# Six small moves in a fused routing attention and mixture-of-experts kernel: sums, gathers, a scatter, first copies and a late value load

## The chip, the cores and the metric

The kernel runs on one core of a Trainium2 chip. The metric is the device time of one execution in microseconds (us). A core has five engines that run side by side and meet at semaphores: TensorE (PE, matmuls), VectorE (DVE), ScalarE (ACT), GpSimd (POOL, which also issues gathers and scatters) and SyncE (SP, which issues loads). Matmuls write to banks of PSUM; everything else lives in SBUF or in device memory.

## The reference, cut to what matters

Two blocks in a row. First, attention in which a query sees only the keys of its own cluster:

```
q, k, v: (4, 8, 768, 64)      centroids: (8, 16, 64)
q_assign = argmax(einsum(q_n, c_n));  k_assign = argmax(einsum(k_n, c_n))
scores   = where(q_assign == k_assign, q @ k.T / sqrt(D), -1e9)
attn_out = softmax(scores) @ v
x        = attn_out as (3072, 512)       # one row for each token
```

Then a mixture of 8 experts, of which each token takes one:

```
logits = x @ w_gate;  e = argmax(logits);  gate = softmax(logits)[e]
y[t]   = gate * (relu(x[t] @ w1[e]) @ w2[e])     # w1: 512x1024, w2: 1024x512 each
```

The tokens of an expert must be brought together (gather), multiplied by that expert's weights, and their rows put back (scatter).

## The kernel before, in words

**Attention.** There are 16 groups: four batches times four pairs of heads. A group has 12 units: two halves of the queries (`half`) by six blocks of 128 keys (`j`). `score(u)` puts a 128x768 tile of scores into one of three wide PSUM tiles (`sps`), ACT takes the exponential into a tile `A` (L1002), and DVE adds the tiles of a half into `T` (`add_up`: L1016 for the first two, L1020 for the rest), for the denominators. `attend(u)` multiplies `A` with the values into one of two banks `O` (L1034). Turn `n` of the main loop does the 12 scores of group `n`, then its 12 attends.

**Jobs between them.** The order of the work is written by hand. `at(n, part, f)` hangs job `f` into turn `n`: a number below 12 is the place behind that score, `UG + j` (with `UG` = 12) the place behind attend `j`, `mid` stands between scores and attends, `end` after the attends. Instructions go onto each engine's queue in exactly this order, and an engine never overtakes within its queue.

**Clusters.** Queries and keys of a group are turned: the first group by PE (`turn`, copied out of PSUM by DVE and ACT at L886, L887 and L891), later groups by DVE alone (`turn_blocks`, L897). `similar(g)` makes the similarities to the centroids on PE (L911) into a wide PSUM tile, which DVE turns (L918). `assign` and `assign2` find the cluster, and its one-hot goes into `ohT` (`put`, `put_q`, `put_by_scalar`), where it masks the scores (L1000). `idle` puts unneeded matmuls on PE while it would wait at the start.

**Experts, in the last turns of attention.** When three batches are done, the tokens of experts 0 and 1 from those batches are placed already. `tokens1` multiplies one-hots on PE into token numbers, which DVE turns into integers (`indices`, L698 to L712). `spread1` spreads these over the partitions (PE L719, DVE L698 to L726, into `g_idx`). `gather1(0)` has POOL fetch nine blocks of rows (L292). Nine of the 12 units of group 14 do not add up at once: they are kept in `later_sums`, which `sums_of_later` works off behind the gathers' issue. In turn 15, `turn_rows1(0)` divides the gathered rows (L305) and turns them (L308) for PE's first layer (L321).

**Experts after attention.** A list `groups` of 15 tiles is worked off: full tiles of experts 2 to 7 by a product scheme with seven half-size products (`layer1_s`, L498; `pair_s`, L520), the others by `layer1` (L321) and `layer2` (L386). Each has its rows gathered (`gather_of`, L292), divided (L305), turned (L308), multiplied, and scattered to the output (`rows_to`, L341). `sums_x` makes the sums of the turned rows (L408, L409) that L498 starts with. `adds[0]` is the postponed tail of a quarter-tile of expert 0: three DVE additions (L367, L371) and a scatter. Weights come as transfers of 2 MB from SP's queue (L236, L241), each when its buffer has been read for the last time.

**The end.** A number `xe[NX + 2]` says whether the inputs need the general path, which these inputs do not take. Every engine loads it into a register (`values_load`, L1460) and branches on it (L1461).

Of the kernel before, what the change touches and what calls it, by code (L numbers as in the profile page):

```python
# [8 lines left out]
F32 = mybir.dt.float32  # L9
# [176 lines left out]
def kernel(  # L186
# [11 lines left out]
    nc = tc.nc  # L198
    B, H, S, D = q.shape
    C = centroids.shape[1]  # L200
    P = 128
# [21 lines left out]
    NX = -(-(N - CAP) // P) + 1  # L223
# [43 lines left out]
    ps_o = late.enter_context(tc.tile_pool(name="ps_o", bufs=2, space=PSUM))  # L267
# [3 lines left out]
    def apart(first, second):  # L271

        first, second = (getattr(i, "ins", i) for i in (first, second))
        tc.declare_no_dep(second, first, reason="other banks and other elements")


    def wide():
        return pools["s"].tile([P, 2, 512], F32, name="sps")
# [4 lines left out]
    def bank():  # L283

        return wide()[:, 0, :] if "attention" in pools else ps_o.tile([P, 512], F32, name="O")

    def gather(g):

        n = 0
        for j, m in enumerate(g["n"]):  # L290
            for i in range(m // 32):
                nc.gpsimd.indirect_dma_start(  # L292
                    out=g["xg"][:, n, :], out_offset=None, in_=x_q[0 : 4 * g["rows"], :],
                    in_offset=bass.IndirectOffsetOnAxis(ap=g["gi"](j, i), axis=0),
                )
                n += 1
# [318 lines left out]
    xe = rte.tile([1, NX + 3], I32)  # L615
# [120 lines left out]
    with ExitStack() as actx:  # L736
# [79 lines left out]
        ps = bank()  # L816
# [44 lines left out]
        def blocks():  # L861
            cps = bank()
            nc.tensor.transpose(cps[:, 0:P], cn.rearrange("p a d -> p (a d)"), ident)
            cview = cps[:, 0:P].rearrange("p (g a c) -> p g a c", a=2, c=C)
            for a in range(2):
                nc.vector.tensor_copy(cblk[a * D : (a + 1) * D, :, a, :], cview[a * D : (a + 1) * D, :, a, :])
# [4 lines left out]
        def turn(g, piece):  # L871

            if piece == 0:
                qk[g] = qkp.tile([P, 2, S], F32, name="qk")
            n = NQ - 4 if piece else 4
            ps = wide().rearrange("p a c -> p (a c)")
            for i in range(2 * n):
                w, j = divmod(i, n)
                if i == n and piece == 0:
                    blocks()  # L880
                nc.tensor.transpose(
                    ps[:, w * 512 + j * P : w * 512 + (j + 1) * P], rows[g, "qk"[w]][:, 4 * piece + j].rearrange("p a d -> p (a d)"), ident
                )
            if piece == 0:
                apart(
                    nc.vector.tensor_copy(qk[g][:, 0, 0:512], ps[:, 0:512]),  # L886
                    nc.scalar.copy(qk[g][:, 1, 0:512], ps[:, 512:1024]),  # L887
                )
            else:
                for w, copy in enumerate((nc.vector.tensor_copy, nc.scalar.copy)):  # L890
                    copy(qk[g][:, w, 512:S], ps[:, w * 512 : w * 512 + n * P])  # L891

        def turn_blocks(g):

            qk[g] = qkp.tile([P, 2, S], F32, name="qk")
            for w in range(2):
                nc.vector.transpose(qk[g][:, w, :], rows[g, "qk"[w]].rearrange("p j a d -> p (j a d)"))  # L897
# [7 lines left out]

        def similar(g):

            ps = wide()[:, 0, :]
            for t in range(4):
                w, half = divmod(t, 2)  # L910
                nc.tensor.matmul(  # L911
                    ps[t * 2 * C : (t + 1) * 2 * C, 0:HS], lhsT=cblk[:, g % HP].rearrange("p a c -> p (a c)"),
                    rhs=qk[g][:, w, half * HS : (half + 1) * HS], start=True, stop=True,
                )


            sims[g] = asg.tile([P, HS], F32, name="sim")
            nc.vector.transpose(sims[g], ps[:, 0:HS])  # L918
# [64 lines left out]
        A, T, O = {}, {}, {}  # L983
        XT = {}

        def where(u):
            g, r = divmod(u, 2 * NQ)
            return g, r // NQ, r % NQ
# [21 lines left out]
        def add_up(u, a_u):  # L1010
            g, half, j = where(u)
            if j == 0:
                last_a[0] = a_u
            elif j == 1:
                T[g, half] = tp_.tile([P, 2, HS], F32, name="T", bufs=4)
                nc.vector.scalar_tensor_tensor(  # L1016
                    T[g, half], in0=last_a[0], scalar=1e-9 / P, in1=a_u, op0=ALU.add, op1=ALU.add
                )
            else:
                nc.vector.tensor_tensor(T[g, half], T[g, half], a_u, op=ALU.add)  # L1020

        later_sums = []

        def sums_of_later():
            for x in later_sums:
                add_up(*x)

        def attend(u):
            g, half, j = where(u)
            if j == 0:  # L1030
                O[g, half] = ps_o.tile([P, 512], F32, name="O")
            a_ = A.pop(u)
            for a in range(2):
                nc.tensor.matmul(  # L1034
                    O[g, half][a * D : (a + 1) * D, 0:HS], lhsT=rows[g, "v"][:, a, j, :], rhs=a_[:, a, :],
                    start=(j == 0), stop=(j == NQ - 1),
                )
# [92 lines left out]
        def at(n, part, f, *a):  # L1130
            jobs.setdefault((n, part), []).append((f, a))

        UG = 2 * NQ
# [10 lines left out]
        at(-3, mid, assign, 0)  # L1144
        at(-3, mid, assign2, 0)
        at(-3, mid, put, 0)
        at(0, 1, put_q, 0, 1)
        at(-2, end, idle_of, 20)
        at(-1, end, turn_blocks, 1)
        for f in (similar, assign, assign2):  # L1150
# [62 lines left out]
        n = NG - HP  # L1213
# [4 lines left out]
        at(n + 1, end, one_hots1, 1)  # L1218

        at(n + 2, UG + 3, tokens1)  # L1220
        at(n + 2, UG + 8, spread1)
        at(n + 2, UG + 8, gather1, 0)
        at(n + 2, UG + 8, sums_of_later)
        at(n + 3, mid, gather1, 1)
        at(n + 3, mid, turn_rows1, 0)

        n = NG
# [54 lines left out]
    with tc.tile_pool(name="sm", bufs=1) as sm:  # L1282
# [20 lines left out]
        for part in parts:  # L1303
            n, over = part["n"], part["over"]
            nc.vector.tensor_tensor(over, over, b2.unsqueeze(2).to_broadcast([P, E, n]), op=ALU.mult)
            more = sm.tile([P, NF], F32, name="more")[:, 0:n]
# [51 lines left out]
    def gather_of(g):  # L1358
        g["xg"] = pools["xg"].tile([P, NJ * 4 + 1, XQ], F32, name="xg")
        gather(g)  # L1360

    def turn_of(g):
        if "xT" not in g:
            g["xT"] = pools["wk"].tile([P, DB, CAP], F32, name="xgT")
        turn_rows(g)
# [7 lines left out]
    def static(e, j0):  # L1373
        c0 = e * (NJ + 1) + j0
        return dict(
            n=[P] * (NJ - j0) + [RQ], rows=N, e=lambda: e, gi=blocks_at(g_idx, c0), si=cols_of(s_idx, c0), apart=True, s=j0 == 0
        )
# [8 lines left out]
    groups = [static(1, 1)]  # L1386
# [3 lines left out]
    ng = len(groups)  # L1390

    def fetch1_of(i):
        groups[i]["e"] = groups[i]["e"]()
        groups[i]["w"] = [fetch1(groups[i]["e"], i + 1)]

    gather_of(groups[0])
    adds[0]()
    gather_of(groups[1])
    groups[0]["w"], groups[1]["w"] = weights[1], w_s
    g = groups[0]  # L1400
    g["xT"] = p1.tile([P, DB, CAP], F32, name="xu", bufs=1)
# [16 lines left out]
    layer2(g)  # L1418
    fetch1_of(2)
    for i, g in enumerate(groups):  # L1420

        n1 = groups[i + 1] if i + 1 < ng else dict(s=False)
        n2 = groups[i + 2] if i + 2 < ng else dict(s=False)
        if i + 1 < ng:
            n1["h"] = pools["wk"].tile([P, FB, CAP], F32, name="h_sb", bufs=2)
            steps = [lambda: divide_rows(n2)] if i + 2 < ng else []
            if i == 0:
                steps.append(lambda: turn_of(n2))
            if n1["s"]:
                layer1_s(n1, steps)  # L1430
            else:
                for f in steps:
                    f()
                layer1(n1, (0, FB))
        if i + 3 < ng:
            fetch1_of(i + 3)
        if i + 2 < ng:
            if i > 0:
                turn_of(n2)
            if i + 4 < ng:  # L1440
                gather_of(groups[i + 4])
        steps = sums_w1(n2) + sums_x(n2) if n2["s"] else []
        if n1["s"]:
            for f in sums_h(n1) + sums_w2(n1):
                f()
        if g["s"]:
            pair_s(g, steps)
            layer2(g, range(2, len(g["n"])))
        else:
            for f in steps:  # L1450
                f()
            if i > 0:
                layer2(g)
        if i + 2 < ng:
            n2["w"].append(fetch2(n2["e"], i + 3))
# [1 line left out]

    mctx.close()
    late.close()
    more = nc.values_load(xe[0:1, NX + 2 : NX + 3], min_val=0, max_val=2)  # L1460
    with tc.If(more > 0):  # L1461
        nx = nc.values_load(xe[0:1, NX : NX + 1], min_val=0, max_val=NX)
        general = nc.values_load(xe[0:1, NX + 1 : NX + 2], min_val=0, max_val=1)
        with tc.If(nx > XU):
            with ExitStack() as ectx:
# [3 lines left out]
                with tc.For_i(XU, nx, 1) as i:  # L1469
# [5 lines left out]
                    g = dict(  # L1475
                        n=[P], rows=N, w=(fetch1(ex, 0), fetch2(ex, 0)), gi=lambda j, i: gi[:, i : i + 1],
                        si=lambda j: gi[:, 4:5], apart=False,
                    )
# [37 lines left out]
```

## Time and profile before

| | us |
|---|---|
| time, median of three (lowest, highest) | 693.03 (692.69, 693.26) |
| span of the profiled execution | 691.1 |
| PE busy | 674.3 |
| DVE busy | 471.8 |
| ACT busy | 310.7 |
| POOL busy | 253.0 |

In the profile's lines, L and a number is the line of the kernel, then come the engine, the operation, the tile written and the tiles read, the shapes and a count. In a timeline the first two numbers are start and duration in us, and a bracket gives how long the engine stood idle before the instruction and what ended that. In a list of waits the numbers are the total in us, how often, and the longest. In the table by stretch, each engine's busy time stands in the order PE, PEld (weight loads of TensorE), DVE, ACT, POOL, followed by the granted clock, the share of the DMA engines that was busy, and GB/s. The end of a matmul is modelled in this profile, not measured.

### The profile page before, as it was taken

What the parts mean: (1) busy time and instruction counts of PE and PEld (TensorE: products, weight loads), DVE (VectorE), ACT (ScalarE), POOL (GpSimd) and SP (SyncE); (2) the same over time, 40 slices, a digit from 0 to 9 for tenths busy, and PEclk for the clock granted to TensorE, in tenths of its full rate; (3) what the DMA queues carried; (4) which work ended last, traced back from release to release, by engine and by line L of the source; (5) the groups of instructions that cost most, each with busy time, mean ns of one, the idle gap of its engine ahead of it and who ended that gap; (6) DMA issues with size and microseconds to landing.
All of it is one profiled execution on the core that took longest, in us unless ns stands there. A gap on an engine that the chain in (4) does not pass through costs nothing.

```text
span 691.1 us, 11981 instructions
## 1 busy us (share of the span) xinstructions
PE 674.3 (98%) x4603; PEld 439.6 (64%) x4603; DVE 471.8 (68%) x740; ACT 310.7 (45%) x470; POOL 253.0 (37%) x327
## 2 busy tenths in 40 slices
PE   8999999999999999999899999999999999999994
PEld 7454444444544444455656779878798787888761
DVE  6987788788898778879666269566765667564200
ACT  3887777778887777786111031211213111131100
POOL 4022222112222221158716764547353563412101
PEclk9999999999999999999999999999999999999998
DMA  8566864988759742521535439686676866668440
GB/s 144 89 93 96 150 141 91 144 165 138 146 53 182 109 79 21 58 37 37 64 124 175 128 113 357 219 278 215 230 272 200 309 200 234 245 231 294 161 139 20
DMA packets 149540, 106.71 MB, mean 154 GB/s; under 512 B 115554, under 2 KB 119650, under 8 KB 149475
## 3 DMA queue, kind: packets, MB, share of 16 engines
q1 hardware_dynamic: 135266, 77.41, 43.8%
q0 software_dynamic: 8640, 19.63, 13.6%
q10 hardware_dynamic: 5568, 8.83, 4.2%
q8 instruction: 38, 0.62, 0.4%
q14 instruction: 28, 0.22, 0.1%
HBM read 93.06 MB, written 13.30 MB: 154 GB/s over the span
## 4 chain that ended last, share of the span: by engine, by line
PE 74%; issue 14%; POOL 7%; DMA 2%; DVE 1%; ACT 1%; ACTq 0%; POOLq 0%; DVEq 0%
PE O L1034 17%; PE sps L997 17%; PE sps L321 9%; PE sps L498 8%; PE sps L386 7%; PE sps L520 5%; POOL xg L292 5%; PE sps L1000 4%; PE sps L1056 2%; POOL out_dram L341 2%; PE sps L911 2%; PE sps L357 1%; PE sps L811 1%; DMA xg<-x_rows,g_idx 1%; DMA wg_in<-in_moe_w_gate_dram 1%
## 5 line engine op out<-in xcount | busy, mean ns | idle before, releaser
L1002 ACT ACTIVATE A<-sps 128x768 f32<-128x768 f32 x192 | 153.6, 810 | 22.1 <-PE sps L1000 20.7
L292 POOL DMA_INDIRECT xg<-x_rows,g_idx x104 | 120.0, 1154 | 116.6 <-DVE xgT L308 81.9
L997 PE MATMUL sps<-qk 64*128 64x384 f32 x768 | 157.1, 487 | 0.1
L1020 DVE TENSOR_TENSOR T<-T,A 128x768 f32<-128x768 f32 x128 | 122.6, 958 | 13.2
L1034 PE MATMUL O<-A,v_in 128*64 128x384 f32 x768 | 127.8, 488 | 0.0
L997 PEld LDWEIGHTS sps<-qk 64*128 64x128 f32 x768 | 67.5, 187 | 49.2 <-issue 44.0
L1034 PEld LDWEIGHTS O<-A,v_in 128*64 128x64 f32 x768 | 53.5, 137 | 67.1 <-issue 65.5
L1000 PE MATMUL sps<-ohT 64*128 64x384 bf16 x384 | 63.5, 322 | 0.0
L341 POOL DMA_INDIRECT out_dram<-zo,s_idx x32 | 37.9, 1183 | 69.7 <-ACT zo L337 31.0
L386 PE MATMUL sps<-w,h_sb 128*128 128x512 f32 x144 | 63.1, 592 | 0.0
L321 PEld LDWEIGHTS sps<-xgT,w 128*128 128x128 f32 x448 | 51.0, 192 | 3.7 <-issue 3.7
L321 PE MATMUL sps<-xgT,w 128*128 128x128 f32 x448 | 51.3, 275 | 0.0
L1087 POOL DMA_DIRECT2D x_rows<-xb x68 | 48.3, 718 | 2.1 <-issue 0.7
L1068 POOL COPY dens<-ls 128x12 f32<-128x12 f32 x16 | 3.2, 203 | 125.1 <-DVE ls L1064 125.1
L929 POOL TENSOR_TENSOR sim<-sim,first_c 128x384 f32<-128x384 f32 x14 | 14.0, 1001 | 91.0 <-DVE sim L928 91.0
L386 PEld LDWEIGHTS sps<-w,h_sb 128*128 128x128 f32 x144 | 26.8, 190 | 30.6 <-issue 30.6
L958 ACT ACTIVATE ohT<-ohs,big 32x384 bf16<-32x384 bf16 x60 | 42.0, 700 | 0.8
L364 ACT COPY zc<-sps 32x512 f32<-32x512 f32 x24 | 13.9, 578 | 60.2 <-PE sps L357 60.1
L498 PEld LDWEIGHTS sps<-xs,w1s 128*128 128x128 f32 x288 | 36.0, 190 | 6.7 <-DVE xs L409 4.2
L498 PE MATMUL sps<-xs,w1s 128*128 128x144 f32 x288 | 37.8, 288 | 1.6 <-issue 1.6
L337 ACT COPY zo<-sps 128x512 f32<-128x512 f32 x12 | 7.0, 585 | 71.3 <-PE sps L386 65.5
L331 ACT ACTIVATE h_sb<-sps 128x512 f32<-128x512 f32 (+1 forms) x18 | 9.6, 578 | 58.1 <-PE sps L321 58.1
(262 smaller groups left out, 951.4 us busy)
## 6 DMA issues: line engine op xcount, KB each, us to landing
w<-in_moe_w_dram SPq DMA_DIRECT2D x28, 2048.0 KB, 9.7
w<-in_moe_w_dram ACTq DMA_DIRECT2D x16, 512.0 KB, 4.5
v_in<-in_v_dram SPq DMA_DIRECT2D x16, 384.0 KB, 3.8
q_in<-in_q_dram SPq DMA_DIRECT2D x60, 96.0 KB, 4.2
k_in<-in_k_dram SPq DMA_DIRECT2D x60, 96.0 KB, 4.9
x_rows<-xb POOLq DMA_DIRECT2D x60, 96.0 KB, 6.3
xg<-x_rows,g_idx POOLq DMA_INDIRECT x104, 3.1
x_rows<-pad SPq DMA_DIRECT2D x64, 3.0 KB, 3.9
```

The costliest lines, as they stand in the source:

```text
L292: nc.gpsimd.indirect_dma_start(out=g["xg"][:, n, :], out_offset=None, in_=x_q[0 : 4 * g["rows"], :], in_offset=bass.IndirectOffsetOnAxis(a ...
L321: nc.tensor.matmul(o, lhsT=g["w"][0][:, c, fb * P : (fb + 1) * P], rhs=g["xT"][:, c, :cols], start=(c == 0), stop=(c == DB - 1),)
L341: ins = nc.gpsimd.indirect_dma_start(out=out[:, :], out_offset=bass.IndirectOffsetOnAxis(ap=g["si"](j)[0:m], axis=0), in_=zo[0:m], in_offs ...
L386: nc.tensor.matmul(zp, lhsT=g["h"][:, fb, j * P : (j + 1) * P], rhs=g["w"][1][:, fb, :], start=(fb == 0), stop=(fb == FB - 1),)
L498: nc.tensor.matmul(o, lhsT=a[:, c, f * P : (f + 1) * P], rhs=b[:, c, :], start=(c == 0), stop=(c == KH - 1),)
L958: nc.scalar.activation(ohT[g][r, 1, cols], t[k], AF.Identity, scale=big[k, a, 0:1], bias=big[k, a, 1:2])
L997: nc.tensor.matmul(ps[:, a, 0:HS], lhsT=qk[g][r, 1, ks], rhs=qk[g][r, 0, qs], start=True, stop=False)
L1000: nc.tensor.matmul(ps[:, a, 0:HS], lhsT=ohT[g][r, 1, ks], rhs=ohT[g][r, 0, qs], start=False, stop=True)
L1002: nc.scalar.activation(A[u], ps[:, :, 0:HS], AF.Exp, scale=D**-0.5)
L1020: nc.vector.tensor_tensor(T[g, half], T[g, half], a_u, op=ALU.add)
L1034: nc.tensor.matmul(O[g, half][a * D : (a + 1) * D, 0:HS], lhsT=rows[g, "v"][:, a, j, :], rhs=a_[:, a, :], start=(j == 0), stop=(j == NQ - 1),)
L1087: nc.gpsimd.dma_start(out=x_d[b * S + c0 : b * S + c1, quad, hp * 32 : (hp + 1) * 32].rearrange("(n t) d -> t n d", t=32), in_=xb[quad * 3 ...
```

## The change

Six edits:

1. The two copies of the second piece of the first group (L891) write different elements from different banks. They are declared independent, as those at L886 and L887 are already.
2. `similar(1)` writes into one of the two `O` banks, which are unused at that time, and leaves the wide tiles to the scores.
3. `put_q(0, 1)`, two ACT copies, moves from behind the second score to behind the third.
4. `sums_of_later` takes a count. Two postponed sums go behind the token numbers of `tokens1`, and the spreading, the gathers and the remaining sums move from behind attend 8 to behind attend 6.
5. The nine gathers of `groups[1]` are issued ahead of `adds[0]`, whose scatter waits for DVE.
6. The number for the end test is loaded ahead of the last tile's second layer, not after all work.

```diff
@@ turn
-                for w, copy in enumerate((nc.vector.tensor_copy, nc.scalar.copy)):
+                apart(*(
                     copy(qk[g][:, w, 512:S], ps[:, w * 512 : w * 512 + n * P])
+                    for w, copy in enumerate((nc.vector.tensor_copy, nc.scalar.copy))
+                ))
@@ similar
-            ps = wide()[:, 0, :]
+            ps = ps_o.tile([P, 512], F32, name="O") if g == 1 else wide()[:, 0, :]
@@
-        def sums_of_later():
-            for x in later_sums:
+        def sums_of_later(n):
+            for x in later_sums[:n]:
                 add_up(*x)
+            del later_sums[:n]
@@
-        at(0, 1, put_q, 0, 1)
+        at(0, 2, put_q, 0, 1)
@@
         at(n + 2, UG + 3, tokens1)
-        at(n + 2, UG + 8, spread1)
-        at(n + 2, UG + 8, gather1, 0)
-        at(n + 2, UG + 8, sums_of_later)
+        at(n + 2, UG + 3, sums_of_later, 2)
+        at(n + 2, UG + 6, spread1)
+        at(n + 2, UG + 6, gather1, 0)
+        at(n + 2, UG + 6, sums_of_later, UG)
@@
     gather_of(groups[0])
+    gather_of(groups[1])
     adds[0]()
-    gather_of(groups[1])
@@
     for i, g in enumerate(groups):
+        if i == ng - 1:
+            more = nc.values_load(xe[0:1, NX + 2 : NX + 3], min_val=0, max_val=2)
@@
     late.close()
-    more = nc.values_load(xe[0:1, NX + 2 : NX + 3], min_val=0, max_val=2)
     with tc.If(more > 0):
```

## The prediction

> **What bounds the kernel now.** I read the page first, then a table of busy time by stretch, then the waits of TensorE, then the timelines around each wait.
>
> ```profile
> PE 674.3 (98%) x4603; PEld 439.6 (64%) x4603; DVE 471.8 (68%) x740; ACT 310.7 (45%) x470; POOL 253.0 (37%) x327
> ```
> ```profile
> 26.80:312.00 285.20, 285.20 (x2204) 139.45 (x2202) 236.61 (x358) 221.94 (x322) 73.04 (x127) 1.00 0.64 104
> 332.30:334.30 2.00, 0.06 (x1) 0.09 (x1) 1.76 (x2) 0.00 (x0) 1.77 (x3) 1.00 0.01 0
> 399.90:401.50 1.60, 0.01 (x1) 0.04 (x1) 1.53 (x4) 1.48 (x3) 0.82 (x1) 1.00 0.08 24
> 401.50:681.00 279.50, 279.49 (x1744) 229.55 (x1744) 158.38 (x221) 51.95 (x90) 115.18 (x100) 1.00 0.66 225
> 681.00:691.10 10.10, 0.00 (x0) 0.00 (x0) 0.00 (x0) 0.59 (x1) 0.97 (x1) 0.73 0.07 25
> ```
>
> The first number after the stretch is its length, the next PE's busy time. PE never stops from 26.8 to 312 nor from 401.5 to 681. So a gain can come only from the start, from the two holes at 332.3 and 399.9, and from the 10.1 us behind the last matmul. PE's own list of waits names the holes:
>
> ```profile
> PE sps L321 <- DVE xu L308: 2.0, 1, 2.0
> PE sps L498 <- issue: 1.6, 1, 1.6
> ```
>
> The DVE timeline ahead of the first hole:
>
> ```profile
> 307.70 0.17 DVE L712 CAST s_idx<-tv 128x4 int32<-128x4 f32 x1
> 310.20 0.17 DVE L698 TENSOR_SCALAR lo<-sps 128x16 f32<-128x16 f32 x1 [2.33 <-PE sps L719]
> 311.18 3.08 DVE L1020 TENSOR_TENSOR T<-T,A 128x768 f32<-128x768 f32 x3
> ...
> 330.80 0.23 DVE L1067 RECIPROCAL rd<-ls 128x12 f32<-128x12 f32 x1
> 331.17 1.51 DVE L305 TENSOR_TENSOR xg<-xg 128x1152 f32<-128x1152 f32 x1
> 332.71 1.38 DVE L308 STREAM_TRANSPOSE xu<-xg 128x1152 f32<-128x1152 f32 x1
> ```
>
> From 310.20 to 334.09 DVE runs with no named idle time; the whole slack stands before it, 2.33 us in which it waits for the spreading matmuls. The division L305 does not wait for the gathers: in the semaphore records the ninth gather's bytes are in at 328.6. So DVE's own queue sets the first hole.
>
> Second hole, from the timeline of 350 to 405:
>
> ```profile
> 374.44 0.95 POOL L292 DMA_INDIRECT xg<-x_rows,g_idx  x1 [0.30 <-issue]
> 376.83 0.68 DVE L371 TENSOR_TENSOR zo<-zc 32x512 f32<-32x512 f32 x1
> 377.79 1.25 POOL L341 DMA_INDIRECT out_dram<-zo,s_idx  x1 [2.40 <-DVE zo L371]
> 379.34 1.75 POOL L292 DMA_INDIRECT xg<-x_rows,g_idx  x1 [0.30 <-issue]
> ...
> 391.17 0.41 SPq L236 DMA_DIRECT2D w<-in_moe_w_dram  x1
> 391.19 0.95 POOL L292 DMA_INDIRECT xg<-x_rows,g_idx  x1 [0.30 <-issue]
> 397.63 1.36 DVE L305 TENSOR_TENSOR xg<-xg 128x1152 f32<-128x1152 f32 x1 [5.97 <-DMA xg<-x_rows,g_idx]
> ```
>
> POOL stands 2.40 us at a scatter, and nine gathers queue behind it. The ninth issues at 391.19, together with a 2 MB weight fetch, and DVE gets its rows only at 397.6. Then L305, L308 and two sums (L408) pass before PE's L498.
>
> **What the Trainium skill says.** "DMA: Bandwidth & Descriptors", section "Issuing engines are not separate DMA queues": transfers from all queues run on the same 16 DMA engines and interleave. The trace agrees: the other gathers of these nine land 2.5 to 2.6 us after their start, the one beside the weight fetch over 6. "SBUF — State Buffer", section "SBUF: two separate sides": a DVE operation with two SBUF inputs and a GpSimd operation that reads SBUF exclude each other on a shared port pair. The trace fits: gathers take 0.94 to 1.71 us beside the sums at 311 to 327 and 0.95 in quiet stretches. "Advanced Engine Details and Errata", section "Engine Queue Depths": 64 for TensorE. Consistent: PE's value load ran at 673.1, while the last matmul began at 680.4. The price of a value load (a floor of about 600 ns in the DMA page, section "Latency and other measured facts") is 0.48 to 0.54 us here; I use the trace's.
>
> **The change, part by part.**
>
> *Two sums early, spreading at 6 instead of 8.* Two L1020 sums cost 2 x 1.06 = 2.1 us (four take 4.15, with a gap of 0.1). They go behind L712, which ends at 307.87, so DVE is busy to 309.97. The spreading matmuls now stand three attends after the token matmuls (attends resume at 306.53 and take 0.66 each), at 308.5, so they wait for nothing and DVE finds their result ready. L698 starts at about 310.05 rather than 310.20: 0.15 us earlier. Behind it 2.1 us of sums are missing. L305 thus can start at 331.17 - 0.15 - 2.12 = 328.9. It also needs the ninth gather: g_idx is 0.15 earlier and DVE as busy as before beside the gathers, so about 328.5, give or take 1 for the lottery of 0.94 against 1.7. L308 ends at 328.9 + 1.54 + 1.38 = 331.8, PE can start at 332.0, and its preceding work lasts to 332.26. The hole of 1.98 closes with 0.26 to spare. I take **1.9**; bounds 1.0 (gathers land 1.2 late) and 2.0. What follows (count, one-hots, tokens) hangs on PE and moves along.
>
> *Gathers of group 1 in front of the scatter.* POOL finishes group 0's gathers at 375.39; the nine can go at 375.7 instead of 379.34, 3.6 us earlier. They then overlap more DVE work (375.4 to 383.8), so I add 1 us of blocked issue: the ninth starts near 388.5 instead of 391.19 and lands by 391.2, ahead of the weight fetch's bytes. DVE is free at 391.66. L305 at 391.8 instead of 397.63 brings the first needed sum to 395.6, 4 us before PE asks at 399.86. Behind the scatter, now nearly 12 us later, stand only another scatter and gathers that are not urgent; its rows are read by nobody on the chip. Gain **1.6**; bounds 0 (the ninth still meets the fetch) and 1.64.
>
> *First copies side by side.* The ACT copy L891 waits 0.60 us for DVE's (9.18 instead of 8.6). The last similarity matmuls then start with the others, at 9.25 instead of 9.61, and the chain to the first scores shortens by 0.36.
>
> *put_q one turn later, similar(1) in an O bank.* PE waits 0.37 at 19.43 for a scores' bank, and two shorter waits follow to 23.4. With three banks for scores alone, 12 scores of 0.81 and one similar of 0.85 take 10.6 us from 15.03 - 0.36, so the attends start at 25.5 to 25.7 instead of 26.84: some 1.2 us. The two scalar copies, 1.03 us, are needed only by the seventh score. But the next thing PE needs from DVE is L897 for group 2, and DVE has no slack there:
>
> ```profile
> 17.82 0.98 DVE L897 STREAM_TRANSPOSE qk<-k_in 128x768 f32<-128x768 f32 x1 [0.42 <-DMA k_in<-in_k_dram]
> ...
> 33.70 0.94 DVE L897 STREAM_TRANSPOSE qk<-k_in 128x768 f32<-128x768 f32 x1
> ```
>
> It starts when group 1's keys land, which no edit moves, and works back to back to 34.64. PE's L911 starts at 34.74. Hence PE would only arrive earlier and wait there, for about 1.1 us, and I count **0.1** of the 1.2. This is the step I am least sure of; its other end is 1.2.
>
> *End test's number loaded early.* Loads move in front of the last expert tile on every engine. PE's queue hides 0.48 us. At the end POOL ran load (681.65 to 682.16), branch and three waits before the increment of its DMA semaphores (682.99, 1.57 us), then a drain of 5.63. The last scatter holds POOL to 682.85 anyhow, so the gain is between 0.14 and 0.51. I take **0.3**.
>
> Sum: 1.9 + 1.6 + 0.1 + 0.3 = 3.9; 693.0 - 3.9 = **689.1**.
>
> **The rivals.** (A) The start pays as well: if DVE's stretch shortens because its sums no longer queue behind late exponentials, 1.1 more: 688.0. Against it: no wait on ACT is named in that stretch. (B) One hole stays: the nine gathers run at 1.6 + 0.3 us each beside the DVE sums, 17.1 us from 375.7, so the ninth issues at 391 and meets the fetch as before; or the gathers of the first hole land late. That keeps 1.0 to 1.6: near 690.6. For it: the gathers' times do scatter. (C) Slower: the load on PE drains its queue (0.5) and the moved sums and gathers only exchange their waits, with 0.4 more on DVE behind blocked ports: 693.9. Against it: PE ran 7 us ahead at its load, and both edits fill idle time that the profile names.
>
> **How the numbers follow.** Forecast 0.62, A 0.12, B 0.18, C 0.08. The range 687.8 to 690.9 takes in A, the spread of the end and most of B. Faster by over 0.2% means under 691.6: forecast, A and nearly all of B, 0.90; within 0.2% 0.05 (both holes half open); slower 0.05.
>
> **What the profile after would show.** PE's waits without L308 and L498; L305 of the first group near 328.9; the ninth gather of the second batch issued before the weight fetch and L305 straight behind the relu; a new wait of PE at similar(2) for DVE L897, near 34.65; POOL's value load before its last scatter. I am wrong if the attends of group 1 start over 0.5 us earlier than 46.5, if PE's wait for L308 or L498 keeps over 0.5 us, or if POOL's drain at the end changes its length.

## The result, and the profile after

The changed kernel takes **688.69 us** (median of six runs, 688.15 to 688.95); the kernel before took 692.92 beside it (692.69 to 693.26). The ratio is 0.9937, with a 95% interval from 0.9924 to 0.9950: 4.2 us less. The forecast was 689.1.

The page, and TensorE's list of waits after the change:

```profile
PE 674.8 (98%) x4603; PEld 440.1 (64%) x4603; DVE 471.8 (69%) x740; ACT 310.6 (45%) x470; POOL 253.6 (37%) x327
```
```profile
PE sps L811 <- POOL ident masks.py:199: 1.4, 1, 1.4
PE sps L386 <- ACT hs L331: 0.6, 1, 0.6
PE sps L914 <- DVE qk L886: 0.6, 1, 0.6
PE sps L914 <- DVE qk L899: 0.2, 1, 0.2
```

No engine works less: PE is busy for 674.8 us (674.3 before), DVE for the same 472. The waits for L308 (2.0 us), at L498 (1.6 us) and, at the start, for an exponential of ACT (0.4 us) have left the list, and a small one for a turn of DVE, L899, has come. The 0.6 us at L386, which the prediction did not count among the places where time could be won, has stayed. (The change shifts the lines: L897 of before is L899 here, L911 is L914, L918 is L921, L1020 is L1023, L1034 is L1038, L1461 is L1467.)

To say where the time went, I cut both spans at the same places:

| stretch | before | after | change |
|---|---|---|---|
| start of the span to DVE's turn of group 1's keys | 17.82 | 18.34 | +0.52 |
| from there to the first attend of group 1 | 28.70 | 28.60 | -0.10 |
| first attend of group 1 to the first attend of group 14 | 256.74 | 256.76 | +0.02 |
| first attend of group 14 to the first L321 | 30.98 | 28.92 | -2.06 |
| first L321 to the last matmul | 346.75 | 345.10 | -1.65 |
| last matmul to the end | 10.08 | 9.50 | -0.58 |

The first row ends, in both profiles, with DVE waiting for the load of these keys, which no edit touches; over the profiles of this study it lies between 16.87 and 18.37. The four rows that the edits touch sum to -4.39, beside -4.2 measured.

Around the **first hole**, DVE's timeline:

```profile
308.14 0.17 DVE L712 CAST s_idx<-tv 128x4 int32<-128x4 f32 x1
308.22 2.01 DVE L1023 TENSOR_TENSOR T<-T,A 128x768 f32<-128x768 f32 x2
310.15 0.17 DVE L698 TENSOR_SCALAR lo<-sps 128x16 f32<-128x16 f32 x1
...
329.00 1.51 DVE L305 TENSOR_TENSOR xg<-xg 128x1152 f32<-128x1152 f32 x1
```

The two sums fill the time in which DVE stood idle ahead of L698, and L698 has lost its bracket. L305 starts at 329.00 in place of 331.17. PE runs into L321 without a gap.

Around the **second hole**, the timeline of all engines:

```profile
387.08 0.95 POOL L292 DMA_INDIRECT xg<-x_rows,g_idx  x1 [0.30 <-issue]
...
389.58 0.41 SPq L236 DMA_DIRECT2D w<-in_moe_w_dram  x1
...
389.59 0.49 DVE L329 TENSOR_SCALAR h_sb<-sps 128x320 f32<-128x320 f32 x1 [3.79 <-PE sps L321]
...
390.00 1.35 DVE L305 TENSOR_TENSOR xg<-xg 128x1152 f32<-128x1152 f32 x1
```

The ninth gather goes 2.5 us ahead of the weight fetch instead of 0.02 behind it, and DVE divides the rows directly after the relu (L329), with no wait for a DMA. The sums for L498 begin at 392.80; PE reaches L498 at 398.20.

The table by stretch, at the places of the two holes (length, then PE's busy time):

```profile
330.00:333.00 3.00, 3.00 (x36) 1.45 (x33) 1.90 (x2) 0.48 (x1) 2.39 (x5) 1.00 0.34 41
396.00:399.00 3.00, 3.00 (x23) 1.22 (x23) 0.00 (x0) 1.16 (x3) 2.10 (x3) 1.00 0.81 305
```

At the **start**, PE's timeline, first before, then after, and behind it the wait of its weight loads for the turn of group 2 after the change (total, times, longest):

```profile
26.85 7.96 PE L1034 MATMUL O<-A,v_in 128*64 128x384 f32 x48
34.74 0.85 PE L911 MATMUL sps<-qk,cblk 128*32 128x384 f32 x8
```
```profile
26.11 7.96 PE L1038 MATMUL O<-A,v_in 128*64 128x384 f32 x48
34.31 1.70 PE L914 MATMUL sps<-qk,cblk 128*32 128x384 f32 x8 [0.24 <-DVE qk L899]
```
```profile
PEld sps L914 <- DVE qk L899: 1.6, 2, 0.9
```

The attends begin 7.77 us after DVE's turn at 18.34. Before they began 9.03 us after it (26.85 - 17.82). So the scores did become some 1.26 us faster (1.17 if counted from the end of the matmuls that turn the first group, L881, on which the arrival of these keys has no bearing). But at `similar(2)`, L914, PE stands 0.24 us for the turned queries, does the half that needs them, and stands again for the keys: the eight matmuls last 1.70 us, against 0.85 before. That gives back 1.09 of the 1.26.

At the **end**, POOL's own instructions, first before, then after. The columns are duration in ns (lowest, median, highest) and start:

```profile
L1460 POOLq TENSOR_LOAD <-xe x1: 509/509/509, 681.7 to 681.7; - x1
L1461 POOLq INC_SWDGE_SEM  x1: 1574/1574/1574, 683.0 to 683.0; - x1
```
```profile
L1467 POOLq COMPARE_BRANCH  x1: 53/53/53, 678.4 to 678.4; - x1
L1467 POOLq INC_SWDGE_SEM  x1: 1574/1574/1574, 679.2 to 679.2; - x1
```

The load now stands at 671.5, and the increment follows the last matmul by 1.42 us instead of 2.00.

### The profile page after: what moved, and what is told of

It reads as the page before. It is cut to its first block, busy times and chain, and to the rows that moved or that the text cites. A ratio compares the mean times of both kernels' runs of the same rounds, so it can differ in the third digit from the quotient of the medians.

```text
span 687.2 us, 11979 instructions
## 1 busy us (share of the span) xinstructions
PE 674.8 (98%) x4603; PEld 440.1 (64%) x4603; DVE 471.8 (69%) x740; ACT 310.6 (45%) x470; POOL 253.6 (37%) x327
## 4 chain that ended last, share of the span: by engine, by line
PE 74%; issue 14%; POOL 6%; DVE 2%; DMA 1%; SPq 1%; POOLq 0%; ACTq 0%; ACT 0%; DVEq 0%
PE sps L1000 17%; PE O L1038 17%; PE sps L321 9%; PE sps L498 8%; PE sps L386 7%; PE sps L520 5%; PE sps L1003 4%; POOL xg L292 3%; PE sps L1060 3%; POOL out_dram L341 2%; PE sps L914 2%; DMA k_in<-in_k_dram 1%; PE sps L357 1%; DVE T L1023 1%; SPq L764 0%
## 5 line engine op out<-in xcount | busy, mean ns | idle before, releaser
L1023 DVE TENSOR_TENSOR T<-T,A 128x768 f32<-128x768 f32 x128 | 122.6, 958 | 13.1
L1038 PE MATMUL O<-A,v_in 128*64 128x384 f32 x768 | 127.8, 488 | 0.0
L1038 PEld LDWEIGHTS O<-A,v_in 128*64 128x64 f32 x768 | 53.6, 137 | 67.0 <-issue 65.0
L386 PE MATMUL sps<-w,h_sb 128*128 128x512 f32 x144 | 63.1, 592 | 0.0
L321 PEld LDWEIGHTS sps<-xgT,w 128*128 128x128 f32 x448 | 51.0, 192 | 3.7 <-issue 3.7
L321 PE MATMUL sps<-xgT,w 128*128 128x128 f32 x448 | 51.3, 275 | 0.0
L386 PEld LDWEIGHTS sps<-w,h_sb 128*128 128x128 f32 x144 | 26.8, 190 | 30.6 <-issue 30.6
L364 ACT COPY zc<-sps 32x512 f32<-32x512 f32 x24 | 13.9, 578 | 60.2 <-PE sps L357 60.0
L498 PEld LDWEIGHTS sps<-xs,w1s 128*128 128x128 f32 x288 | 36.0, 190 | 5.0 <-DVE xs L409 4.2
L498 PE MATMUL sps<-xs,w1s 128*128 128x144 f32 x288 | 37.9, 288 | 0.0
```

Source lines behind the costliest of these rows:

```text
L321: nc.tensor.matmul(o, lhsT=g["w"][0][:, c, fb * P : (fb + 1) * P], rhs=g["xT"][:, c, :cols], start=(c == 0), stop=(c == DB - 1),)
L386: nc.tensor.matmul(zp, lhsT=g["h"][:, fb, j * P : (j + 1) * P], rhs=g["w"][1][:, fb, :], start=(fb == 0), stop=(fb == FB - 1),)
L498: nc.tensor.matmul(o, lhsT=a[:, c, f * P : (f + 1) * P], rhs=b[:, c, :], start=(c == 0), stop=(c == KH - 1),)
L1038: nc.tensor.matmul(O[g, half][a * D : (a + 1) * D, 0:HS], lhsT=rows[g, "v"][:, a, j, :], rhs=a_[:, a, :], start=(j == 0), stop=(j == NQ - 1),)
```

## The experiments

All ratios are to the kernel before, measured together with the kernel in question on the same chip. The kernels come in three sets. In the first (e1 to e4) the kernel before takes 693 us. In the second (e5, e6, e7, e9) and third (e8, e10 to e12) it takes 709 to 710 us: PE pauses there, and TensorE's granted clock falls from 1.00 to 0.50 for some us at a time, mostly between 392 and 428 us. Totals of those two sets are good to 1 to 2 us only, and I read their kernels mainly by the stretches ahead of that one.

**e1: edit 4 alone** (two sums early, spreading at 6).

```diff
+        at(n + 2, UG + 3, sums_of_later, 2)
-        at(n + 2, UG + 8, spread1)          # and gather1, sums_of_later
+        at(n + 2, UG + 6, spread1)          # and gather1, sums_of_later
```

> The kernel before with edit 4 alone (two sums behind the token numbers, spreading behind attend 6). Theory (DVE's queue makes the hole of 1.98 us ahead of L321, and the sums fill its idle 2.33 us): the hole closes, 1.9 to 2.0 us faster than before, ratio 0.9972. Rival (the gathers' landing sets the hole, and it moves by only 0.15 to 0.4 us): under 0.5 us faster, and PE keeps over 1.5 us of waiting for L308.

691.00 us against 693.17, ratio 0.9971 [0.9962, 0.9980]. The first hole is gone, L305 starts at 328.87, and from group 14's attends to L321 it is 28.93 us. TensorE's longest wait is now the other hole:

```profile
PE sps L498 <- issue: 1.6, 1, 1.6
```

**e2: edit 5 alone** (nine gathers ahead of the scatter).

```diff
+    gather_of(groups[1])
     adds[0]()
-    gather_of(groups[1])
```

> The kernel before with edit 5 alone (gathers of group 1 ahead of the scatter that waits for DVE). Theory (the ninth gather met the weight fetch): the hole of 1.64 us ahead of L498 closes, 1.6 us faster, ratio 0.9976, and L305 of that group starts within 0.5 us of the relu ahead of it. Rival (the nine gathers only run slower beside DVE, and the ninth still meets the fetch): no change, hole kept.

691.13 us, ratio 0.9970 [0.9960, 0.9979]. The other hole is gone and this one stays:

```profile
PE sps L321 <- DVE xu L308: 2.0, 1, 2.0
```

Three of its gathers take 1.68 to 2.11 us for their issue beside DVE's additions, the rest 0.95; L305 starts at 392.11, straight behind the relu.

**e3: edits 1 to 3 alone** (the start).

> The kernel before with edits 1 to 3 alone (the start). Theory (DVE works back to back from the landing of group 1's keys to the turn for group 2, so PE arrives earlier and waits there): 0.0 to 0.2 us faster, and PE shows a new wait for the turn at similar(2) of about 1 us. Rival (the scores and their banks set the start): 1.2 us faster, ratio 0.9983, without that wait.

692.32 us, ratio 0.9991 [0.9980, 1.0001]. That interval excludes neither a gain of zero nor the rival's 1.2 us, so the trace must decide. From DVE's turn to group 1's attends it is 28.60 us, against 28.70, and the wait that was expected at `similar(2)` is there, as matmuls that last 1.58 us and not 0.85:

```profile
33.08 1.58 PE L913 MATMUL sps<-qk,cblk 128*32 128x384 f32 x8
```

In this profile DVE's turn of group 1's keys begins 0.83 us earlier than in that of before, with its loads, so its span says nothing on the edits; the distance does.

The 0.10 holds for the keys' arrival in the profile of before. In the other profiles with the old start the distance is 28.66 to 28.67 (e2, e4, e6), but 29.01 (e12), 29.07 (e1) and 29.19 (e9) in those whose keys were turned soon after the queries; with the new start it is 28.60 or 28.61 in all that have nothing else changed there. In e1 and e7 this turn begins at nearly the same time (17.77 and 17.72), and the distances are 29.07 and 28.61. So edits 1 to 3 are worth 0.1 us or less where the keys come late and, as an estimate from e12, e1 and e9 beside e7, 0.4 to 0.6 where they come early.

**e4: edit 6 alone** (the early load).

> The kernel before with edit 6 alone (end test's number loaded ahead of the last tile). Theory (the load and the steps behind it stand in POOL's own order ahead of the semaphore increment, whatever the scatter does): 0.5 to 0.6 us faster, from the last matmul to the end 9.5 us and not 10.1. Rival (the last scatter's rows or POOL's busy time set the end): 0.0 to 0.15 us faster, the stretch stays over 9.9 us.

692.76 us, ratio 0.9996 [0.9983, 1.0009]. That is too coarse for half a microsecond, so the stretch decides: from the last matmul to the end 9.50 us, against 10.06 to 10.08 in every profile with the old load.

The four changes to the stretches, 2.05 (e1), 1.68 (e2), 0.10 (e3) and 0.58 (e4), sum to 4.41; all together gave 4.39. In these stretches the edits do not help or hinder each other.

**e5: the changed kernel with one sum of group 0 behind the turn of group 2**, and **e6: the same on the kernel before.** This asks whether DVE sets the start.

```diff
+            if u == UG - 1:
+                last_of_0.append((u, A[u]))        # added behind turn_blocks(2)
...
+                if g == 0:
+                    at(0, mid, sum_of_0)
```

> The changed kernel, and the last sum of group 0 (one L1023, 1.06 us) goes behind the turn of group 2's queries and keys on DVE's queue, into the idle 0.94 us that DVE had there. Theory (that turn alone holds PE at similar(2)): PE reaches group 1 about 1.0 us earlier; from the start of the turn of group 1's keys to the first attend of group 1 27.6 us, where the changed kernel has 28.6; 1.0 us faster than the changed kernel, ratio to the kernel before 0.992. Rival (PE's and ACT's own work sets the start): 28.6 stays, no gain over the changed kernel.

> The kernel before with the same one sum moved, without the six edits. Theory (without edits 1 to 3 PE reaches similar(2) only when the turn ends anyhow): 0.0 to 0.1 us faster, the stretch from the turn of group 1's keys to group 1's attends stays at 28.6 to 28.7. Rival (DVE alone bounds the start, edits 1 to 3 do nothing): 1.0 us faster, the stretch falls to 27.6.

e5: 701.90 us, ratio 0.9897 [0.9879, 0.9916]; the distance falls from 28.60 to 27.78. e6: 709.76 us, ratio 1.0006 [0.9992, 1.0020]; the distance stays at 28.66. PE at `similar(2)` in e5, then in e6:

```profile
33.51 0.85 PE L914 MATMUL sps<-qk,cblk 128*32 128x384 f32 x8
```
```profile
26.57 7.96 PE L1040 MATMUL O<-A,v_in 128*64 128x384 f32 x48
34.46 0.85 PE L911 MATMUL sps<-qk,cblk 128*32 128x384 f32 x8
```

With the change's faster scores, taking 1.06 us out of DVE's way makes L914 short and waitless. Without them it does nothing: in e6 DVE is through its turn at 33.31, and PE comes from its attends only at 34.46.

**e7: the changed kernel without the two early sums** (the spreading stays at 6).

```diff
-        at(n + 2, UG + 3, sums_of_later, 2)
```

> The changed kernel without the two early sums: spreading and gathers stay behind attend 6, all sums come behind them. Theory (the hole ahead of L321 is DVE's queue): only the 1.3 us by which the spreading comes earlier are taken from DVE's idle time, so a hole of 0.5 to 0.8 us comes back, 0.6 us slower than the changed kernel. Rival (the earlier gathers closed the hole): no hole, same time.

704.07 us, ratio 0.9924 [0.9908, 0.9940]. A part of the hole is back:

```profile
PE sps L321 <- DVE xu L308: 0.7, 1, 0.7
```

L698 starts at 308.77 here, but L305 only at 329.75, because DVE has the two sums still before it.

**e8: the changed kernel with the spreading back at 8**, the two early sums kept.

```diff
-        at(n + 2, UG + 6, spread1)          # and gather1, sums_of_later
+        at(n + 2, UG + 8, spread1)
```

> The changed kernel with the spreading, the gathers behind it and the remaining sums put back from two turns earlier to the old place; the two early sums stay. Theory (the two sums taken out of VectorE's queue behind the spreading close the hole, the earlier place of the spreading is hardly needed): L698 starts at most 0.3 us later than in the changed kernel, TensorE's wait ahead of L321 stays under 0.3 us, time within 0.3 us of the changed kernel. Rival (the earlier spreading is what frees the path): L698 and with it the gathers and L305 come 1.3 us later, a hole of 0.7 to 1.3 us ahead of L321 is back, time 0.7 to 1.3 us over the changed kernel.

703.90 us, ratio 0.9920 [0.9892, 0.9948], beside 703.00 for the changed kernel in the same set (e10), with runs that overlap (701.55 to 704.08 against 702.51 to 703.48). No wait of PE ahead of L321, and 28.93 us from group 14's attends, as with the change. DVE:

```profile
310.17 0.17 DVE L698 TENSOR_SCALAR lo<-sps 128x16 f32<-128x16 f32 x1 [0.40 <-PE sps L719]
...
329.03 1.51 DVE L305 TENSOR_TENSOR xg<-xg 128x1152 f32<-128x1152 f32 x1
```

After the two sums L698 waits 0.40 us, and that is all that the earlier spreading buys: counted from group 1's attends, L698 comes 0.46 us later than in e10 and L305 0.47 later, a little more than the 0.3 expected. The hole had been closed with more room than that. The rival (1.3 us of hole) falls.

**e9: the kernel before, but the 2 MB weight fetch that met the ninth gather issued from ScalarE's queue.** The scatter still stands ahead of the gathers.

```diff
-        nc.sync.dma_start(out=w1, in_=moe_w1[bass.ds(e, 1)].rearrange("e (a p) f -> p (e a) f", p=P))
+        (queue or nc.sync).dma_start(out=w1, in_=moe_w1[bass.ds(e, 1)].rearrange("e (a p) f -> p (e a) f", p=P))
...
-        groups[i]["w"] = [fetch1(groups[i]["e"], i + 1)]
+        groups[i]["w"] = [
+            fetch1(nc.scalar.value_load(xe[0:1, 0:1], min_val=0, max_val=E - 1), i + 1, nc.scalar)
+            if i == 2 else fetch1(groups[i]["e"], i + 1)
+        ]
```

> The kernel before, in its order of gathers and scatter, but the first-layer weights of the tile two further on are fetched from ACT's queue behind the copies of the tile before, some 10 us later. Theory (the ninth gather was late because it met that fetch): it lands 2.6 us after its issue, L305 starts 3.5 us earlier, the hole of 1.64 us ahead of L498 closes: 1.6 us faster than before, unless the weights then come late for their own matmuls, which would show as a new wait of PE at L321. Rival (POOL's order alone made it late): L305 and the hole stay.

708.67 us, ratio 1.0004 [0.9987, 1.0021]. The fetch goes out some 24 us later than before, where 10 were expected, because ACT first stands 15.35 us ahead of a copy (L364). ACT's queue, POOL, DVE and PE in its timelines:

```profile
415.55 0.40 ACTq L236 DMA_DIRECT2D w<-in_moe_w_dram  x1
```
```profile
392.88 0.95 POOL L292 DMA_INDIRECT xg<-x_rows,g_idx  x1 [0.30 <-issue]
```
```profile
395.55 1.36 DVE L305 TENSOR_TENSOR xg<-xg 128x1152 f32<-128x1152 f32 x1 [3.53 <-DMA xg<-x_rows,g_idx]
```
```profile
400.14 1.12 PE L498 MATMUL sps<-xs,w1s 128*128 128x144 f32 x7
```

The ninth gather goes even later than before (392.88 against 391.19), yet DVE has its rows 2.67 us after the issue instead of 6.44, and L498 follows the matmuls ahead of it (they end at 400.21) with no gap. e6, measured in the same set with the fetch in its old place, has the rows 6.59 us after the issue (392.81, 399.40) and a hole of 3.06 us ahead of L498. So the collision made the second hole, not the late issue alone.

The time did not follow. In this kernel PE then has pauses of 9.0 us in all at L498, nearly all between 402 and 416 us, for which the profile names no wait ("issue"), and one of 1.5 us for DVE's L367, which stood behind the late L364. e6 has 6.0 us of unnamed pauses there, between 416 and 424 us.

**e10, e11, e12: the changed kernel, e5 and e9 once more, measured together with e8.**

> The changed kernel as it is, beside the other three on one chip, so that they can be set against it. Both theories: 0.6% under the kernel before (4.2 us), attends of group 1 begin 28.6 us after VectorE's turn of group 1's keys starts, no wait of TensorE for L308 or for the gate's first matmul over 0.5 us.

> The changed kernel with one 1.06 us sum of group 0 moved behind the turn of group 2. Theory (VectorE's stretch from group 1's keys to the turn of group 2 sets the start): the distance from the first turn to group 1's attends falls from 28.6 to 27.7 and the time by 0.8 to 1.0 us against the changed kernel on the same chip, some 5.1 us (0.74%) under the kernel before. Rival (TensorE or the arrival of keys sets the start, so a shorter VectorE stretch is given back later): distance may fall, time within 0.3 us of the changed kernel.

> The kernel before with its scatter still ahead of the gathers, but with the 2 MB weight fetch that met the ninth gather moved to ScalarE's queue, some 20 us later. Theory (the second hole came from the gather and the fetch sharing the transfer engines): the ninth gather lands 2.6 us after its issue instead of over 6, the hole of 1.6 us ahead of L498 is gone, time 1.4 to 1.7 us under the kernel before, unless the fetched weights then come late for their own matmuls, which would show as a wait of TensorE for a DMA at L321 or L498. Rival (POOL's late issue alone makes the hole): the hole keeps over 1 us and the time stays.

e10: 703.00 us, ratio 0.9917 [0.9891, 0.9943]; the stretches repeat (28.60, 28.93, 9.50). What is different in this set: PE stops for 3.87 us in front of an L386 that waits for DVE's relu (L329), a wait that the profile after doesn't have and that the expectation did not name, and the granted clock drops. The clock is the number third from the end (a mean: it is 0.50 from 395.7 to 402.5 us and 1.00 on both sides):

```profile
396.70 6.56 PE L386 MATMUL sps<-w,h_sb 128*128 128x512 f32 x8 [3.87 <-DVE h_sb L329]
```
```profile
395.00:405.00 10.00, 8.30 (x24) 2.94 (x24) 4.79 (x7) 1.02 (x2) 4.19 (x5) 0.66 0.66 237
```

e11: 702.04 us, ratio 0.9915 [0.9886, 0.9945]: the medians are 1.0 apart as the theory has it, but the runs overlap (701.61 to 704.97 against 702.51 to 703.48), so in total time it is not shown to beat the changed kernel. Its distance is 28.17, only 0.43 shorter. The turn of group 2 ends at 32.69, and PE comes from its attends at 33.25: here PE itself is already the bound, as it was by less in e5 (33.24 and 33.51).

e12: 709.82 us, ratio 1.0008 [0.9991, 1.0025]. Again no hole ahead of L498, and DVE's L305 follows the ninth gather's issue by 2.61 us; again nothing in the total. No wait for a DMA is named behind it, so late weights are not seen; 9.7 us of pauses without a named cause are, and 1.5 us for L367 as in e9. In both runs nearly all of these pauses lie ahead of the moved fetch's issue (415.55 in e9, 419.31 in e12), so they are not waits for its weights. What they come from, and whether they swallow the gain, stays open.

## Why the prediction was right, step by step

**Two sums and spreading: forecast 1.9, measured 2.05 to 2.06.** Right in mechanism and nearly in size. L698 at 310.05 was forecast, 310.15 came; L305 at 328.9, 329.00 came. As group 1's attends begin 0.42 us later in this profile (46.94 against 46.52), both in fact came 0.3 us earlier within the work than forecast, which is room and no time: the hole was closed. The forecast named the two sums as the main part and gave 0.15 us to the earlier spreading. e8 confirms that: with the spreading at its old place, the whole gain is there. e7 shows the counterpart: without the sums, the earlier spreading brings 1.3 of it, because the sums then run behind it. Either edit works on the same hole, and the sums alone close it.

**Gathers ahead of the scatter: forecast 1.6, measured 1.65 to 1.68.** The ninth gather was forecast for 388.5 and went at 387.08; the work there lies 1.64 us earlier than before already, by edit 4 and this profile's late start (2.06 - 0.42), so from batch to ninth gather the forecast was right within 0.2. Three gathers took 1.17, 0.73 and 1.01 us longer than 0.95. They run beside two-input additions of DVE, which fits what the Trainium skill says ("SBUF — State Buffer", section "SBUF: two separate sides"); the lock itself is not seen in a trace, and a fourth gather, at 379.78, took 0.95 us beside such an addition. Rival B let all nine be blocked; three were. That the hole came from the weight fetch on the same transfer engines was argued from the trace of before and from "DMA: Bandwidth & Descriptors", section "Issuing engines are not separate DMA queues". e9 and e12 show that the fetch is the cause: with it moved, the rows of a gather issued late are still used 2.6 to 2.7 us later. That shared engines are the way it acts is what the page says.

**Start: forecast 0.1 of a possible 1.2, measured 0.10.** This was the least sure step, and its mechanism held. The scores end 1.17 to 1.26 us earlier (1.2 forecast), and 1.09 is lost at `similar(2)` (1.1 forecast). The exact hit owes something to luck: with keys that come early the old start takes 0.4 to 0.6 us more than the new one (e12, e1 and e9 beside e7), so the premise that DVE sets the old start held for the arrival in the profile of before and not for every run. One sum of the forecast does not come out either: 15.03 - 0.36 + 10.6 is 25.3, not the 25.5 to 25.7 that it took; in the profile after it is 11.04 us from the first score to the attends (15.07 to 26.11) instead of 10.6. e5 and e6 together show why little of the faster scores reaches the time: they and the shorter way through DVE are each worth 0.1 us or less alone where the keys come late, and together they bring 0.82 more. The other end, rival A, would have needed a shorter stretch on DVE, and none of the six edits shortens it. The wait takes another form than I wrote. I had PE wait once, near 34.65; it waits for the queries, works, and waits again for the keys, so that most of the loss hides in a longer L914.

**Early load: forecast 0.3, measured 0.58, over my upper bound of 0.51.** The step that failed is "The last scatter holds POOL to 682.85 anyhow". After the change the increment starts at 679.15, while the last scatter's span on POOL lasts to 679.59 (678.62 + 0.97). The increment therefore does not wait for that span. On POOL's queue before, the load started at 681.65 and the branch at 682.23: 0.58 us, all of which the end gains. The drain keeps its 5.63 us. The bound of 0.51 was the load's own duration, without the step to the next instruction.

The sum was 3.9, and 4.2 came. The term that was mis-sized is the last; the first was 0.15 short. Of the three signs that would have made me wrong, none came: group 1's attends start at 46.94, no wait of PE for L308 or at L498 is left, and the drain has the same length.

## What to carry to other kernels

Read each engine's gap by the work that ends last ahead of it, and look for idle time of that same engine shortly before: two postponed sums that had stood behind the critical job paid 2.06 us by filling a wait in front of it. Where two engines each hold up the same instruction, an edit that speeds one of them shows little in the time and is still half of a gain; the distance between two fixed instructions tells that where the total cannot, if it is read over several profiles, because the first of the two can itself move with a load. A small gather that is needed soon should go ahead of a large transfer, not beside it.

## What was not expected of the hardware

- The span that the profile draws for a scatter on POOL does not hold POOL's later control instructions: the semaphore increment began 0.44 us before the span's end, and by as much in every profile with the early load.
- The same kernel before took 693 us in one set and 709 to 710 in the two others, more than all six edits together bring. In e10 the stretch from the first L321 to the last matmul took 360.3 us instead of 345.1, while the stretch from group 1's attends to group 14's agrees within 0.02 us (256.78 and 256.76). In these traces the granted clock is either 1.00 or 0.50. By the profile's times, in which the ends of matmuls are modelled, each of the 16 drops ahead of the last matmul begins 2 to 7 us after PE has begun to pause: in e10 PE stands still from 392.83 us, and the clock falls at 395.7. So the traces do not show the low clock as what starts the pauses. What does, and why in those two sets, was not tried.
- A hole can cost more than its length. In the profile of e4, in the first set, the hole ahead of L498 lasts 2.01 us; the clock is 0.50 for the next 3.4 us, in which the table counts 16 matmuls of PE where it counts 30 in the profile of before (below, in this order), and from the first L321 to the last matmul it takes 348.80 us instead of 346.75. Of these 2.05 us only 0.37 are the longer hole. The hole of 1.98 us in the profile of before has no such drop behind it.

```profile
402.10:405.50 3.40, 3.40 (x16) 3.40 (x16) 2.93 (x6) 0.00 (x0) 2.51 (x3) 0.50 0.25 61
402.10:405.50 3.40, 3.40 (x30) 3.40 (x30) 2.58 (x5) 0.64 (x1) 2.79 (x3) 1.00 0.28 65
```

- From the first L321 to the last matmul e6, which still has its second hole's cause, and e10, which has not, take 360.4 and 360.3 us in their profiles. A hole in PE's work may cost nothing where PE pauses anyhow directly behind it; one profile of each is too little to show it.
